# Sliding-window attention and a low-rank mixer on one core: Q and K transposed on the vector engine, scores by 64-key blocks on row tiles, batch 0 mixed d-major with a PE-added mask, loads in order of need

## The chip, the cores and the metric

The kernel runs on one core of a Trainium2 chip. The metric is the device time of one execution in microseconds (us); lower is better. A kernel was run several times, beside runs of the kernel before on the same chip, and the median is quoted. Most runs count as "fast". A run more than 1.5% above the fastest of the same kernel counts as "slow" and is left out of every comparison of times.

Engines: PE is the tensor engine (matmuls), PEld its weight loads, DVE the vector engine, ACT the scalar engine, POOL GpSimd, which issues the loads here. PSUM is the memory that PE writes its results to. "Granted clock" is the clock that the throttle gave PE, as a part of full speed.

## The reference, cut to what matters

```python
# q, k, v: (8 batches, 8 heads, 576 positions, 64), f32
scores = q @ k.T / 8                      # per batch and head
mask   = (0 <= i - j) & (i - j < 64)      # causal window of 64 positions
x      = softmax(where(mask, scores, -1e9)) @ v      # -> (8, 576, 512)
u      = x + (x.T @ U @ V).T              # U (576, 32), V (32, 576): mixes positions, low rank
out    = u + relu(u @ w_ch1) @ w_ch2      # (512, 2048) and (2048, 512)
```

There are 4608 tokens. The two large products (the MLP) work on 9 chunks of 512 tokens. A block of 64 queries sees 128 keys at most, so the attention is small, but its scores and its product with V need many small matmuls.

## The kernel before: the parts that the argument touches

All of it is one static schedule. Batch 0's attention runs alone first (the "preamble", filled up with idle matmuls). Then nine MLP chunks follow. The attention of batch c+1 is cut into pieces, and these are put by hand into the slots between the MLP steps of chunk c.

Q and K come token-major from memory and must be turned so that the head dimension lies on partitions. Before, PE does it, and ACT and DVE copy the result out of PSUM:

```python
def tr(src, j, wide=False):
    ...                                   # cut: batches 0 and 1, transposes of 96 x 96
    tp = ps_tp.tile([P, NT, P], BF16, name="tpn", tag="tp")
    for t in range(NT):                   # NT = 5; 8 calls a batch: 40 transposes
        nc.tensor.transpose(tp[:, t, :], src[:, t, 2*j : 2*j+2, :]..., ident[:])
    return ...
def TK(j): nc.scalar.copy(out=like(kt[j][:]), in_=tr(kb, j))
def TQ(j): nc.vector.tensor_copy(out=like(qt[j][:]), in_=tr(qb, j, ...))
```

The scores of a block of 64 queries are taken against a pair of key blocks (128 keys, 128 output rows), then exponentiated on ACT and multiplied by a 0/1 mask on DVE:

```python
def scores(sc, n, j, blk):
    w0 = 0 if blk == 0 else W * (blk - 1)
    for g in range(2):                    # two heads, on the two halves of PE's rows
        nc.tensor.matmul(sc[:, g, n*W:(n+1)*W],
                         kt[j][rs, w0 : w0 + P], qt[j][rs, blk*W:(blk+1)*W], ...)
def SC(j):
    ...
    nc.scalar.activation(out=dst, in_=sc[:], func=ACT.Exp, scale=scale)
    nc.vector.tensor_tensor(out=dst, in0=dst, in1=maskA..., op=ALU.mult)
```

After the low-rank product with U, batch 0 makes u token-major and turns it back, piece by piece, before the first MLP matmul can start (V: 5 products and adds, UT: transposes and copies):

```python
for part, n in (("PV", 2), ("U", 0), ("V", 0), ("UT", 0)):
    for f in a[part]:
        f()
        turn_over(n, 256)                 # idle matmuls
```

V is loaded twice, the second time shifted by 64 rows. The order of the loads is Q/K of batch 0, V of batch 0, w1, w2, then Q/K and V of batch 1.

The softmax here doesn't subtract the row's maximum and nothing guards it: scores larger than these inputs give would overflow.

Of the kernel before, what the change touches and what calls it, by code (L numbers as in the profile page):

```python
# [9 lines left out]
ALU = mybir.AluOpType  # L10
# [6 lines left out]
def kernel(  # L17
# [19 lines left out]
    HP = H // 2  # L37
# [3 lines left out]
    GR = 6  # L41
    NGR = 2
    GP = S // GR
# [14 lines left out]
    kg_pool = ctx.enter_context(tc.tile_pool(name="kg", bufs=4))  # L58
# [6 lines left out]
    ps_tp = ctx.enter_context(tc.tile_pool(name="ps_tp", bufs=1, space=bass.MemoryType.PSUM))  # L65
    first = ExitStack()
    psum = {
        "mm": first.enter_context(tc.tile_pool(name="ps_t0", bufs=2, space=bass.MemoryType.PSUM)),
        "spare": first.enter_context(tc.tile_pool(name="ps_s0", bufs=1, space=bass.MemoryType.PSUM)),
# [4 lines left out]

    ident = const.tile([P, P], BF16, name="ident")
    maskA = const.tile([P, 2, NB - 1, W], BF16, name="maskA")
    w1b = const.tile([P, NDC, F], BF16, name="w1b")
    w2b = const.tile([P, NFC, DM], BF16, name="w2b")
    NT = 5
    uf = [const.tile([P, NT, R], FP32, name=f"uf{i}") for i in range(2)]  # L80
    ub = [const.tile([P, NT, R], BF16, name=f"ub{i}") for i in range(2)]
    vrep = const.tile([P, W + S + W], BF16, name="vrep")
    vf = const.tile([P, S], FP32, name="vf")
# [3 lines left out]
    vB = [const.tile([P, NFULL, H, VW], BF16, name=f"vB{i}") for i in range(2)]  # L87
    kn = [const.tile([P, NT, H, D], BF16, name=f"kn{i}") for i in range(2)]
    qn = [const.tile([P, NT, H, D], BF16, name=f"qn{i}") for i in range(2)]
    kt = [const.tile([P, S], BF16, name=f"kt{j}") for j in range(HP)]  # L90
    qt = [const.tile([P, S], BF16, name=f"qt{j}") for j in range(HP)]
    pts = const.tile([P, HP, 2, NB, W], BF16, name="pts")

    loaded = {}


    def load_kq(b, split):
        grouped = b < NGR
        if grouped:
            kb = kg_pool.tile([GP, H, GR, D], BF16, name="kg")  # L100
            qb = kg_pool.tile([GP, H, GR, D], BF16, name="qg")
        else:
            kb, qb = kn[b % 2], qn[b % 2]
        loaded[b] = (kb, qb)
        if grouped:
            step = 2 if split else H
            for h0 in range(0, H, step):
                hs = slice(h0, h0 + step)
                for t, src in ((kb, k), (qb, q)):
                    nc.gpsimd.dma_start(  # L110
                        out=t[:, hs, :, :].rearrange("p h c d -> p h (c d)"),
                        in_=src[b, hs, :, :].rearrange("h (p c) d -> p h (c d)", c=GR),
                    )
                    yield
        else:
            for t in range(NT):
                rows = P if t < NFULL else W
                for dst, src in ((kb, k), (qb, q)):
                    nc.gpsimd.dma_start(  # L119
                        out=dst[0:rows, t, :, :],  # L120
                        in_=src[b, :, t * P : t * P + rows, :].rearrange("h p d -> p h d"),
                    )
                yield

    def load_v(b, both=False):
        va, vb = vA[b % 2], vB[b % 2]
        for t in range(NFULL):
            nc.gpsimd.dma_start(  # L128
                out=va[:, t, :, 0:D],
                in_=v[b, :, t * P : (t + 1) * P, :].rearrange("h p d -> p h d"),  # L130
            )
            if both and t > 0:
                nc.gpsimd.dma_start(  # L133
                    out=vb[:, t - 1, :, 0:D],
                    in_=v[b, :, t * P - W : t * P + W, :].rearrange("h p d -> p h d"),
                )
        lo = 0 if both else W
        nc.gpsimd.dma_start(
            out=vb[lo:P, NFULL - 1, :, 0:D],
            in_=v[b, :, NFULL * P - W + lo : S, :].rearrange("h p d -> p h d"),  # L140
        )

    def shift_v(b, copy):
        va, vb = vA[b % 2], vB[b % 2]
        for t in range(NFULL):
            if t > 0:
                copy(out=vb[W:P, t - 1, :, 0:D], in_=va[0:W, t, :, 0:D])
            copy(out=vb[0:W, t, :, 0:D], in_=va[W:P, t, :, 0:D])


    kq0 = load_kq(0, True)
    nc.vector.memset(idle[:], 0.0)  # L152
    nc.vector.memset(ident[:], 0.0)
    next(kq0)
    next(kq0)
# [9 lines left out]
    nc.vector.memset(maskA[:, 0, 0:2, :], 1.0)  # L165
    for _ in kq0:
        pass

    for n, base, step, mult in ((0, 0, 1, -1), (1, -1, -1, 1), (1, W, 1, -1)):
        nc.gpsimd.affine_select(  # L170
            out=maskA[:, 0, n, :],
            in_=maskA[:, 0, n, :],
            compare_op=ALU.is_ge,
            fill=0.0,
            base=base,
            pattern=[[step, W]],
            channel_multiplier=mult,
        )
    for i in range(2):
        nc.vector.memset(vA[i][:, :, :, D:VW], 1.0)  # L180
        nc.vector.memset(vB[i][:, :, :, D:VW], 1.0)
# [3 lines left out]
    nc.vector.memset(uf[0][:, NT - 1, :], 0.0)  # L185
    nc.vector.memset(uf[1][:, 0, :], 0.0)
    nc.vector.memset(xs[0][W:P, NT - 1, :, :], 0.0)
    nc.vector.memset(xs[1][0:W, 0, :, :], 0.0)
    for i in range(2):
        nc.vector.memset(kn[i][W:P, NFULL, :, :], 0.0)  # L190
        nc.vector.memset(qn[i][W:P, NFULL, :, :], 0.0)


    nc.sync.dma_start(
        out=uf[0][:, 0:NFULL, :], in_=moe_U[0 : NFULL * P, :].rearrange("(c p) r -> p c r", p=P)
    )
    nc.sync.dma_start(out=uf[0][0:W, NFULL, :], in_=moe_U[NFULL * P : S, :])
    nc.sync.dma_start(out=uf[1][W:P, 0, :], in_=moe_U[0:W, :])
    nc.sync.dma_start(
        out=uf[1][:, 1:NT, :], in_=moe_U[W:S, :].rearrange("(c p) r -> p c r", p=P)  # L200
    )
    for g in range(4):
        nc.sync.dma_start(out=vf[g * R : (g + 1) * R, :], in_=moe_V[:, :])
    w1v = moe_w_ch1.rearrange("(c p) n -> p c n", p=P)
    for lo, hi in ((0, 1024), (1024, 2048)):
        nc.gpsimd.dma_start(out=w1b[:, :, lo:hi], in_=w1v[:, :, lo:hi])
    shift_v(0, nc.gpsimd.tensor_copy)
    w2v = moe_w_ch2.rearrange("(i p) m -> p i m", p=P)
    for lo, hi in ((0, 8), (8, 16)):
        nc.gpsimd.dma_start(out=w2b[:, lo:hi, :], in_=w2v[:, lo:hi, :])  # L210
    for _ in load_kq(1, False):
        pass
    load_v(1, both=True)
# [10 lines left out]
    def attention(b, spare=False, alone=False):  # L224
        odd = b % 2
        kb, qb = loaded[b]
# [5 lines left out]
        grouped = b < NGR  # L232
        turn = [0]

        def tr(src, j, wide=False):
            if grouped:
                if spare and turn[0] % 3 != 0:
                    tpb = psum["mm"].tile([P, 2 * CH], BF16, name="tpm", tag="mm")
                    tp = tpb[:, 0:S].rearrange("d (c p) -> d c p", c=GR)
                elif wide:  # L240
                    tpw = ps_big.tile([P, 2, 2 * CH], BF16, name="tpw", tag="big")
                    tp = tpw[:, 0, 0:S].rearrange("d (c p) -> d c p", c=GR)
                else:
                    tp = ps_tp.tile([P, GR, GP], BF16, name="tpg", tag="tp")
                turn[0] += 1
                for c in range(GR):
                    for g in range(2):
                        nc.tensor.transpose(
                            tp[g * D : (g + 1) * D, c, :], src[:, 2 * j + g, c, :], ident[0:GP, 0:GP]
                        )  # L250
                return tp.rearrange("d c p -> d p c")
            tp = ps_tp.tile([P, NT, P], BF16, name="tpn", tag="tp")
            for t in range(NT):
                nc.tensor.transpose(  # L254
                    tp[:, t, :],
                    src[:, t, 2 * j : 2 * j + 2, :].rearrange("p h d -> p (h d)"),
                    ident[:],
                )
            return tp.rearrange("d t p -> d (t p)")[:, 0:S]

        def like(ap):
            return ap.rearrange("d (p c) -> d p c", c=GR) if grouped else ap

        def TK(j):
            def f():
                nc.scalar.copy(out=like(kt[j][:]), in_=tr(kb, j))
            return f

        def TQ(j):
            def f():  # L270
                nc.vector.tensor_copy(out=like(qt[j][:]), in_=tr(qb, j, alone and not spare))
            return f

        def scores(sc, n, j, blk):
            w0 = 0 if blk == 0 else W * (blk - 1)
            for g in range(2):
                rs = slice(g * D, g * D + D)
                nc.tensor.matmul(  # L278
                    sc[:, g, n * W : (n + 1) * W],
                    kt[j][rs, w0 : w0 + P],  # L280
# [325 lines left out]
```

## Time and profile before

Three runs before the prediction gave 350.76 to 352.54 us, median 351.7. The profiled run has a span of 349.8 us.

| part | us | what it is |
|---|---|---|
| MLP of one chunk alone | 27.6 | chunk 7, in which nothing else runs |
| preamble | 28.5 | until the first MLP matmul |
| chunks 0 and 1 | 40.2, 41.0 | with the attention of batches 1 and 2, and all first loads |
| chunks 2 to 5 | 36.5 to 37.0 | with one batch's attention and the next batch's transposes |
| chunk 6 | 34.2 | one batch's attention, no transposes |

These lines are from the page of the kernel before: PE's busy time, share and instructions; the bytes; and the chain of work that ended last, by engine.

```profile
PE 332.9 (95%) x2963; PEld 167.0 (48%) x3014; DVE 174.5 (50%) x320; ACT 125.0 (36%) x191; POOL 119.5 (34%) x150
...
HBM read 43.57 MB, written 9.44 MB: 152 GB/s over the span
...
PE 82%; DMA 9%; POOL 4%; issue 2%; ACT 1%; DVE 1%; POOLq 0%; ACTq 0%
```

PE is busy nearly throughout (95% of the span), so work that leaves PE should shorten the time. The windows view of the kernel before, cut at the first MLP matmul of each chunk, gives for each stretch its length, the busy time of PE, PEld, DVE, ACT and POOL (with instruction counts), then the granted clock, the mean DMA share and GB/s:

```profile
0.00:28.52 28.52, 22.64 (x314) 11.47 (x319) 16.16 (x43) 12.03 (x18) 22.81 (x37) 1.00 1.30 165
28.52:68.71 40.19, 37.80 (x394) 19.00 (x400) 21.29 (x36) 14.72 (x22) 25.03 (x29) 1.00 2.21 180
68.71:109.72 41.01, 38.60 (x374) 20.80 (x379) 21.14 (x40) 16.75 (x26) 33.89 (x40) 1.00 2.45 148
109.72:146.36 36.64, 36.22 (x338) 18.71 (x343) 20.10 (x36) 15.11 (x23) 15.39 (x18) 1.00 1.06 93
146.36:182.82 36.46, 36.15 (x334) 18.47 (x339) 19.92 (x36) 14.52 (x22) 15.39 (x18) 1.00 1.04 89
...
256.24:290.44 34.20, 33.84 (x298) 16.39 (x302) 18.50 (x32) 12.65 (x19) 0.00 (x0) 1.00 0.09 32
```

Chunk 6 (the last line) does an attention like that of chunk 3 (the fifth) but no transposes of a next batch, and is 2.26 us shorter. The timeline of PE in chunk 3 shows one group of transposes and two pieces of the scores (start, duration, operation, tiles, tile shape, count):

```profile
149.04 0.41 PE L278 MATMUL sc<-qt_115,kt_111 64*128 64x64 bf16 x16
149.29 0.40 PE L278 MATMUL sc<-qt_116,kt_112 64*128 64x64 bf16 x16
149.62 3.67 PE L435 MATMUL psA<-uTc,w1b 128*128 128x512 bf16 x15
...
164.28 0.45 PE L254 MATMUL tpn<-ident,kn_108 128*128 128x128 bf16 x5
164.57 0.38 PE L457 MATMUL psU<-w2b,c_4_2310 128*128 128x512 bf16 x1
```

From start to start, five transposes take 0.29 us (164.28 to 164.57), and eight such groups make 2.3 us a batch. The 32 score matmuls take 0.58 us (149.04 to 149.62), 18 ns each, weight load included.

### The profile page before, as it was taken

The page shows a single profiled execution, that of the slowest core. Times are in us where ns is not written, and L with a number is a line of the kernel's source. Part 1 is how long each engine was busy: PE and PEld are TensorE (multiplying, and loading weights), DVE is VectorE, ACT ScalarE, POOL GpSimd, SP SyncE. Part 2 cuts the span into 40 slices and gives each one's busy share as a digit, 9 for nine tenths or more (in the row PEclk, how much of TensorE's full clock was granted, in tenths as well). Part 3 has the DMA queues.
Part 4 walks back from the last instruction along what each step waited for, and adds up shares of the span by engine and source line. Part 5 has one row for each costly group of instructions (what it writes and reads, how often), then busy time and mean ns, then how long its engine had stood idle before and what let it go on. Part 6 is the DMA issues. An engine that isn't in the chain of part 4 may idle for free.

```text
span 349.8 us, 7003 instructions
## 1 busy us (share of the span) xinstructions
PE 332.9 (95%) x2963; PEld 167.0 (48%) x3014; DVE 174.5 (50%) x320; ACT 125.0 (36%) x191; POOL 119.5 (34%) x150
## 2 busy tenths in 40 slices
PE   7978989988999999999999999999999999999995
PEld 3434454444554455545554555445544454444442
DVE  3574257555653755375446545664546554214311
ACT  2632461355332632354225423353335231401300
POOL 8892269989944046605480160000000000000000
PEclk9999999999999999999999999999999999999999
DMA  8999999999999059906995292000010011011011
GB/s 112 166 207 207 198 142 188 167 171 143 149 127 167 2 37 134 187 24 45 108 163 66 15 131 66 32 2 30 32 62 0 32 43 49 0 60 62 0 52 69
DMA packets 132175, 31.89 MB, mean 91 GB/s; under 512 B 121264, under 2 KB 126384, under 8 KB 132144
## 3 DMA queue, kind: packets, MB, share of 16 engines
q0 software_dynamic: 125552, 21.57, 88.7%
q1 hardware_dynamic: 6592, 9.88, 8.2%
q8 instruction: 23, 0.38, 0.4%
q14 instruction: 8, 0.07, 0.1%
HBM read 43.57 MB, written 9.44 MB: 152 GB/s over the span
## 4 chain that ended last, share of the span: by engine, by line
PE 82%; DMA 9%; POOL 4%; issue 2%; ACT 1%; DVE 1%; POOLq 0%; ACTq 0%
PE psU L457 34%; PE psA L435 31%; DMA qg<-in_q_dram 6%; PE tpn L254 5%; PE xr L324 3%; DMA vA_103<-in_v_dram 2%; PE sc L278 2%; PE psv L373 2%; PE tpu L408 2%; PE pshh L353 1%; POOL kg L110 1%; ACT pts L293 1%; POOL qg L110 1%; POOL vA_103 L128 1%; POOL w2b L210 0%
## 5 line engine op out<-in xcount | busy, mean ns | idle before, releaser
L435 PE MATMUL psA<-uTc,w1b 128*128 128x512 bf16 x553 | 129.8, 379 | 2.1 <-ACT uTc L413 0.7
L435 PEld LDWEIGHTS <-w1b 128*128 128x128 bf16 x576 | 54.0, 98 | 62.6 <-issue 2.2
L466 DVE TENSOR_TENSOR osb<-psU,un 128x512 f32<-128x512 f32 x36 | 24.8, 690 | 60.5 <-PE psU L457 54.2
L293 ACT ACTIVATE pts<-sc 128x1024 bf16<-128x1024 f32 x32 | 31.4, 1023 | 17.9 <-PE sc L278 17.9
L294 DVE TENSOR_TENSOR pts<-pts,maskA 128x1024 bf16<-128x1024 bf16 x32 | 22.2, 695 | 17.8 <-ACT pts L293 17.6
L128 POOL DMA_DIRECT2D vA_104<-in_v_dram x16 | 14.2, 889 | 43.7 <-PE xr L324 35.7
L413 ACT COPY uTc<-tpu 128x512 bf16<-128x512 bf16 x27 | 15.8, 585 | 27.9 <-PE tpu L408 27.9
L128 POOL DMA_DIRECT2D vA_103<-in_v_dram x16 | 14.3, 907 | 17.0 <-PE xr L324 16.5
L333 DVE RECIPROCAL rcp<-xr 128x8 f32<-128x8 f32 (+1 forms) x40 | 8.2, 204 | 21.4 <-PE xr L324 21.2
L324 PEld LDWEIGHTS <-pts 128*64 128x64 bf16 x576 | 12.8, 110 | 12.2 <-issue 9.5
L119 POOL DMA_DIRECT2D kn_108<-in_k_dram x15 | 13.0, 866 | 9.0 <-PE tpn L254 8.5
L389 DVE TENSOR_TENSOR un<-psv,xs_102 128x512 bf16<-128x512 f32 (+1 forms) x18 | 11.9, 687 | 7.9 <-PE psv L373 7.9
L408 PEld LDWEIGHTS <-un 128*128 128x128 bf16 x144 | 10.6, 98 | 8.9 <-issue 1.9
L389 DVE TENSOR_TENSOR un<-psv,xs_101 128x512 bf16<-128x512 f32 (+1 forms) x18 | 11.5, 682 | 5.8 <-PE psv L373 5.8
L334 DVE TENSOR_TENSOR xs_102<-xr,rcp 128x512 bf16<-128x512 f32 (+1 forms) x20 | 13.8, 692 | 0.7
L334 DVE TENSOR_TENSOR xs_101<-xr,rcp 128x512 bf16<-128x512 f32 (+1 forms) x20 | 13.8, 690 | 0.7
L500 PE MATMUL unread<-idle 128*128 128x256 bf16 (+1 forms) x46 | 12.5, 371 | 1.6 <-DVE idle L152 1.3
L119 POOL DMA_DIRECT2D kn_107<-in_k_dram x15 | 12.9, 863 | 3.2 <-PE tpn L254 2.5
L119 POOL DMA_DIRECT2D qn_110<-in_q_dram x15 | 13.1, 874 | 1.4 <-PE tpn L254 1.4
L119 POOL DMA_DIRECT2D qn_109<-in_q_dram x15 | 13.0, 867 | 1.2 <-PE tpn L254 0.9
L373 PE MATMUL psv<-hh,vrep 128*128 128x512 bf16 x40 | 12.7, 379 | 0.7 <-DVE un L389 0.6
L133 POOL DMA_DIRECT2D vB_106<-in_v_dram x12 | 10.7, 892 | 6.2 <-DMA w2b<-in_moe_w_ch_dram 4.2
(579 smaller groups left out, 590.8 us busy)
## 6 DMA issues: line engine op xcount, KB each, us to landing
out_dram<-osb SPq DMA_DIRECT2D x36, 256.0 KB, 2.6
vA_103<-in_v_dram POOLq DMA_DIRECT2D x16, 128.0 KB, 6.0
w1b<-in_moe_w_ch_dram POOLq DMA_DIRECT2D x2, 1024.0 KB, 13.7
w2b<-in_moe_w_ch_dram POOLq DMA_DIRECT2D x2, 1024.0 KB, 15.3
vA_104<-in_v_dram POOLq DMA_DIRECT2D x16, 128.0 KB, 5.7
vB_106<-in_v_dram POOLq DMA_DIRECT2D x16, 128.0 KB, 5.9
kn_107<-in_k_dram POOLq DMA_DIRECT2D x12, 128.0 KB, 5.5
qn_109<-in_q_dram POOLq DMA_DIRECT2D x12, 128.0 KB, 5.6
```

The lines of the kernel that those rows point to most:

```text
L119: nc.gpsimd.dma_start(out=dst[0:rows, t, :, :], in_=src[b, :, t * P : t * P + rows, :].rearrange("h p d -> p h d"),)
L128: nc.gpsimd.dma_start(out=va[:, t, :, 0:D], in_=v[b, :, t * P : (t + 1) * P, :].rearrange("h p d -> p h d"),)
L293: nc.scalar.activation(out=dst, in_=sc[:], func=ACT.Exp, scale=scale)
L294: nc.vector.tensor_tensor(out=dst, in0=dst, in1=maskA.rearrange("p g n w -> p g (n w)"), op=ALU.mult)
L324: nc.tensor.matmul(xr[r0 : r0 + W, h // 4, (h % 4) * VW : (h % 4 + 1) * VW], pts[:, h // 2, h % 2, blk, :], rhs, start=True, stop=True,)
L334: nc.vector.tensor_tensor(out=x[lo:hi, t, :, :].rearrange("p (a h) d -> p a h d", a=2), in0=xv[:, :, :, 0:D], in1=rcp[lo:hi].to_broadcast( ...
L373: nc.tensor.matmul(ps[:, n, :], vrep[:, off : off + P], hh["sb"][:], start=True, stop=not on_pe)
L389: nc.vector.tensor_tensor(out=u_tiles[g][rs, :], in0=ps[rs, n, :], in1=xt[n][rs], op=ALU.add)
L408: nc.tensor.transpose(tp[:, dc, :], u_tiles[g][:, dc * P : (dc + 1) * P], ident[:])
L435: nc.tensor.matmul(ps[:], w1b[:, dc, i * P : (i + 1) * P], uTc[:, dc, :], start=(dc == 0), stop=(dc == NDC - 1),)
L457: nc.tensor.matmul(acc[t][:], c1[i][:, t * P : (t + 1) * P], w2b[:, i, :], start=(i == 0), stop=(i == NFC - 1),)
L466: nc.vector.tensor_tensor(out=osb[:], in0=acc[t][:], in1=u_tiles[g][:], op=ALU.add)
```

## The change

The intent is to take everything off PE that another engine can do, and to start the MLP sooner:

1. Q and K are loaded in runs such that DVE's transpose instruction (STREAM_TRANSPOSE in the profile; the kernel arranges its operands in blocks of 32x32) gives the wanted layout. PE's transposes and the copies out of PSUM go.
2. The scores are taken by single 64-key blocks, against up to 128 queries at once: 80 matmuls a batch on 64x64 tiles instead of 72 on 64x128.
3. Batch 0's mask is added in PSUM by PE before the exponential. Batch 0's result is built d-major in PSUM (features on partitions, as the MLP needs it: x transposed plus the product of V and the low-rank part), so that no turning back is needed; its token-major u follows in chunk 0.
4. V is loaded once, and shifted by copies on DVE. Loads are issued in order of need.

The diff, cut to its core:

```diff
-        tp = ps_tp.tile([P, NT, P], BF16, name="tpn", tag="tp")
-        for t in range(NT):
-            nc.tensor.transpose(tp[:, t, :], src[:, t, 2*j : 2*j+2, :]..., ident[:])
+    def KT(x, n):                        # batches 0 and 1: as pairs, in 32-bit elements
+        if pair:
+            nc.vector.transpose(out=dst[...].bitcast(U32)..., in_=src[...].bitcast(U32)...)
+        else:
+            nc.vector.transpose(out=dst[:, n * S : (n + 1) * S]..., in_=src[...]...)
 ... (cut)
+    def SC0(n):                          # batch 0: mask first, on PE
+        for g in range(2):
+            nc.tensor.matmul(sc[:, g, 0 : PB * W], ident[:], bias[...], start=True, stop=False)
+        ...                              # then the scores, accumulated onto it
+    def SC(n):
+        if alone:
+            return SC0(n)
+        for r in range(max(len(x) for x in todo)):
+            for e in range(ne):          # ne = 2 where Q/K lie as pairs (batch 1), else 1
+                for half in range(2):
+                    jj, kb, a, z = todo[half][r]
+                    for g in range(2):
+                        nc.tensor.matmul(
+                            sc[half * W : (half + 1) * W, g, (a - lo) * W : (z - lo) * W],
+                            operand("k", g, jj, e, kb * W, (kb + 1) * W),
+                            operand("q", g, jj, e, ...), ...)
 ... (cut)
+    def XT(t):   # x transposed into PSUM, left open
+    def UP():    # plus (low-rank part) @ V, then four copies to the MLP's operand
 ... (cut)
-    DVE_RELU = (1, 2, 3, 5, 6, 7, 9, 11)
+    DVE_RELU = (1, 4, 7, 10, 13)
 ... (cut: new slots)
+    PLACE   = {"VC": [0], "S": [1, 1, 4, 4, 7, 7], "PV": [10, 10, 13, 13, 15],
+               "KT": [8, 9, 11, 12, 14, 16, 18, 19], ...}
+    PLACE_1 = {"KT": [14, 15, 17, 18], "S": [17, 17, 19, 19, 21, 21], "VC": [23], ...}
+    KT_3    = [22, 23, 24, 25, 26, 27, 29, 30]
+    turn_over(88, P)                     # idle matmuls of 128 columns at the start
 ... (cut)
+            place(b + 1, ("KT",), {"KT": KT_3} if b == 2 else PLACE)
```

"KT" is the list of slots of the DVE transposes of the next batch. In the last line, chunk 1 places batch 3's transposes late (slots 22 to 30), and all later chunks use slots 8 to 19.

## The prediction

> **What bounds the kernel now.** The page gives PE 95% busy at full granted clock; the chain that ended last is 82% PE. In the timeline MLP matmuls (128x512) follow each other every 0.216 us, so a chunk of 128 costs 27.6 us. Nine chunks are 249 of the 349.8 us span, untouched by the change. The rest, by stage (windows view):
> - preamble (batch 0's attention), to the first MLP matmul: 28.5 us, bound by dependencies and DMA. From the last low-rank matmul (22.6) to that MLP matmul it is 5.5 us.
> - chunks 0 and 1: 40.0 and 41.4 us, 12 to 14 above the floor.
> - chunks 2 to 5: 36.4 to 37.0 us each; chunk 6: 34.2; chunks 7 and 8: the floor, plus a 4 us tail.
> Chunk 6 differs from 2-5 only in having no Q/K transposes of a next batch, so these cost PE about 2.3 us a batch (40 transposes, start to start 55 ns: 2.2 us).
>
> **What changes.**
> 1. Q/K transposes leave PE for DVE. Gain 2.2 us in each of chunks 2-5, about 4.5 in chunk 1, which does two batches. New: 8 DVE transposes of 576 elements. [...] Removed: 4 q copies (0.45 us) on DVE, 4 k copies on ACT (0.65), three of eight DVE relus (0.69). Added: V shifts, about 1.5 us. [...]
> 2. Scores: 72 matmuls of 64 columns (1.7 us of PE a batch) become 80, mostly of 128 columns, on four 64x64 tiles. If four run at once [...], PE cost stays 1.5-2 us; if only two do, 2.8.
> 3. V is loaded once, not twice; Q and K descriptors become 512 B, or 4.6 KB for batches 0 and 1 (but from batch 2 each byte of Q and K is fetched twice).
> 4. Batch 0: 4 Q/K loads instead of 8, no PE transposes or PSUM copies, mask in PSUM, result built d-major, so after U come hh copy, 4 matmuls and 2 copies per engine: about 2.2 us instead of 5.5. MLP starts near 22 instead of 28.5. Its u adds (5 matmuls, 1.1 us) move into chunk 0.
> 5. Loads in order of need: batch 1's Q/K (landed at 45.2 us now, and waited for) come before the second half of w2; I estimate 37 us at the 0.4 MB/us that w2 reached.
>
> **Sum.** Preamble -6.5, chunk 0 -2.5, chunk 1 -5, chunks 2-5 -1.8 each = -7, chunk 6 +0.3: about -21 us, nearly all on the critical path, because PE is the chain there. The ideal without new waits is -24. Predicted 331 us, 8 in 10 between 324 and 340. Chances: faster 0.95, within 2% 0.04, slower 0.01.
>
> **What would show it.** First MLP matmul at 21-23 us; chunks 2-5 of 34.3-35.2 us; [...] no PE waits over 0.5 us after chunk 1; the DMA share near full through chunks 0 and 1; two score pieces taking 0.5-0.65 us between MLP matmuls.
>
> **What would make it wrong.** Batch 2's Q/K (4.7 MB of reads, each DMA writing only 32 partitions) landing late, so that DVE blocks in order behind its transposes and chunk 1 waits 5 us or more; w1 or w2 late, since MLP starts 6.5 us sooner with the same bytes to fetch; transposes twice as slow; score tiles running in pairs only (+1 us a batch).

The sum came to about -21 us (-6.5, -2.5, -5, -7, +0.3); DVE's work entered it only in that DVE was taken not to be a bound. Measured, a bf16 transpose took 0.79 us in the mean, and DVE's busy time in chunks 2 and 3 went from 20.10 and 19.92 to 24.45 and 23.18 us. The V shifts, an estimate of 1.5 us, took 1.65 (0.68 and 0.97 at 100.51). The 1.5-2 and 2.8 us for the scores are estimates (from start to start a batch took 1.37 us before and takes 1.40 now); that four tiles run at once was an assumption, which e11 tests.

## The result, and the profile after

| kernel | median us | lowest to highest | runs |
|---|---|---|---|
| before | 351.92 | 350.76 to 352.54 | 4 |
| after | 336.47 | 335.85 to 337.35 | 4 |

The ratio is 0.9562, with a 95% interval of 0.953 to 0.9595: faster. Ratios here and below compare fast runs, and are not quite the ratio of the medians.

The prediction of 331 us (324 to 340) holds the measured 336.47. The gain was 15.4 us and not 21. That the range held it owes something to its width of 16 us: stage by stage, as the table below shows, misses of 10.3 us stood against 3.5 us more than predicted elsewhere. The page of the kernel after, the lines that answer those of before:

```profile
PE 317.6 (95%) x2848; PEld 156.1 (47%) x2891; DVE 195.8 (58%) x343; ACT 118.3 (35%) x188; POOL 87.9 (26%) x116
...
HBM read 51.30 MB, written 9.44 MB: 181 GB/s over the span
...
PE 57%; DMA 29%; DVE 7%; POOL 3%; issue 2%; ACT 0%; DVEq 0%; POOLq 0%
```

PE's busy time fell by 15.3 us and the span by 14.1. V is read once, but from batch 2 on Q and K are read twice, so 51.3 MB are read instead of 43.6. The chain that ended last now goes through DMA for 29%, against 9%. That is not the price of the bytes: e1 below reads the same 51.3 MB, and DMA has 2% of its chain. It is the wait of chunk 2, shown next, that leads the chain back into the loads. The windows view of the kernel after, in the same columns:

```profile
0.00:25.79 25.79, 20.88 (x392) 15.48 (x393) 15.98 (x42) 7.80 (x10) 17.93 (x32) 1.00 1.29 163
25.79:65.76 39.97, 36.82 (x389) 17.75 (x396) 26.41 (x43) 12.89 (x21) 17.38 (x21) 1.00 1.72 185
65.76:99.68 33.92, 33.39 (x301) 16.14 (x306) 27.42 (x47) 13.57 (x22) 16.71 (x20) 1.00 2.48 161
99.68:138.80 39.12, 35.84 (x309) 16.79 (x311) 24.45 (x41) 14.88 (x24) 17.05 (x21) 0.96 2.24 151
138.80:173.01 34.21, 33.77 (x302) 16.14 (x306) 23.18 (x40) 13.71 (x22) 14.67 (x18) 1.00 1.49 149
...
242.19:276.33 34.14, 33.88 (x306) 16.39 (x310) 18.37 (x32) 14.29 (x23) 0.00 (x0) 1.00 0.09 32
```

Set side by side, with the terms of the prediction (stage lengths in us, after minus before; "c0" is chunk 0):

| | preamble | c0 | c1 | c2 | c3 to c5 | c6 | c7, c8 | sum |
|---|---|---|---|---|---|---|---|---|
| predicted | -6.5 | -2.5 | -5 | -1.8 | -5.4 | +0.3 | 0 | -21 |
| measured, this profile | -2.73 | -0.22 | -7.09 | +2.48 | -6.49 | -0.06 | 0 | -14.1 |

Chunks 1 and 3 to 5 did better than predicted. The preamble, chunk 0 and chunk 2 fell short, by 3.8, 2.3 and 4.3 us. So three questions are left: what keeps the preamble long, what eats the gain of chunk 0, and why chunk 2 alone is 5 us longer than its like.

In the preamble, PE's timeline of the kernel after shows a hole that no dependence explains:

```profile
18.19 0.20 PE L375 MATMUL xr<-vA,pts 128*64 128x65 bf16 x1
20.17 0.33 PE L588 MATMUL xT<-idle 128*128 128x128 bf16 x3 [1.79 <-issue]
...
25.79 1.46 PE L513 MATMUL psA<-uTc,w1b 128*128 128x512 bf16 x6 [0.61 <-DVE uTc L492]
```

PE stands 1.79 us before an idle matmul on constant data. "issue" says that the profile knows nothing that it waited for.

In chunk 2, DVE's timeline of the kernel after shows a real wait:

```profile
111.50 0.82 DVE L243 STREAM_TRANSPOSE kt<-kr 128x576 bf16<-128x576 bf16 x1 [1.16 <-DMA vB<-in_v_dram]
114.05 0.81 DVE L243 STREAM_TRANSPOSE qt<-qr 128x576 bf16<-128x576 bf16 x1 [1.72 <-DMA qr<-in_q_dram]
```

And PE's timeline of the same microseconds:

```profile
116.44 0.22 PE L375 MATMUL xr<-vA,pts 128*64 128x65 bf16 x1 [2.02 <-DVE xs L385]
117.41 0.22 PE L375 MATMUL xr<-vA,pts 128*64 128x65 bf16 x1 [0.52 <-DVE xs L385]
```

DVE runs its instructions here in the order of the program. At 111.5 and 114.05 it stands before transposes of batch 4, which nobody needs until the next chunk (the last K load of batch 4 landed at 111.31 and the last Q load at 113.83 us; that the profile names V's DMA at 111.5 is its guess), and behind them wait a relu and the scaling of x ("xs") that PE needs for the current batch. The windows view of these microseconds shows what PE made of it, and what the clock did then:

```profile
114.00:118.00 4.00, 1.46 (x35) 0.79 (x34) 3.82 (x8) 0.21 (x1) 1.62 (x2) 1.00 2.69 124
118.00:120.00 2.00, 1.82 (x5) 0.69 (x5) 1.97 (x5) 0.49 (x1) 0.81 (x1) 0.53 2.36 151
```

PE was busy for 1.46 of 4 us, and in the next 2 us the granted clock was 0.53: six MLP matmuls took 2.69 us from start to start (118.36 to 121.05), 0.45 us each and not 0.216. The stall is paid for twice.

### The profile page after: what moved, and what is told of

The parts are those of the page before. It is cut to its first block, busy times and chain, and to the rows that moved or that the text cites. A ratio compares the mean times of both kernels' runs of the same rounds, so it can differ in the third digit from the quotient of the medians.

```text
span 335.7 us, 6763 instructions
## 1 busy us (share of the span) xinstructions
PE 317.6 (95%) x2848; PEld 156.1 (47%) x2891; DVE 195.8 (58%) x343; ACT 118.3 (35%) x188; POOL 87.9 (26%) x116
## 4 chain that ended last, share of the span: by engine, by line
PE 57%; DMA 29%; DVE 7%; POOL 3%; issue 2%; ACT 0%; DVEq 0%; POOLq 0%
PE psU L535 27%; PE psA L513 24%; DMA qr<-in_q_dram 13%; DMA vA<-in_v_dram 12%; DMA kr<-in_k_dram 4%; PE xr L375 2%; PE sc L341 2%; PE tpu L451 2%; DVE un L431 2%; DVE qt L243 2%; DVE xs L385 1%; DVE osb L544 1%; POOL kr L112 1%; PE pshh L401 1%; PE psv L420 1%
## 5 line engine op out<-in xcount | busy, mean ns | idle before, releaser
L535 PE MATMUL psU<-w2b,c 128*128 128x512 bf16 x558 | 133.2, 379 | 1.7 <-issue 1.0
L524 ACT ACTIVATE c<-psA 128x512 bf16<-128x512 f32 x99 | 59.3, 599 | 100.5 <-PE psA L513 99.9
L535 PEld LDWEIGHTS <-c 128*128 128x128 bf16 x576 | 53.3, 98 | 59.9 <-issue 3.3
L522 DVE TENSOR_SCALAR c<-psA 128x512 bf16<-128x512 f32 x45 | 30.7, 682 | 36.6 <-PE psA L513 36.5
L124 POOL DMA_DIRECT2D vA<-in_v_dram x32 | 29.0, 911 | 46.5 <-PE xr L375 26.8
L349 ACT ACTIVATE pts<-sc 128x768 bf16<-128x768 f32 x42 | 31.7, 808 | 12.5 <-PE sc L341 10.6
L456 ACT COPY uTc<-tpu 128x512 bf16<-128x512 bf16 x30 | 17.6, 585 | 41.0 <-PE tpu L451 41.0
L356 DVE TENSOR_TENSOR pts<-pts,mask 128x768 bf16<-128x768 bf16 x42 | 23.3, 558 | 11.8 <-ACT pts L349 8.3
L385 DVE TENSOR_TENSOR xs<-xr,rcp 128x512 bf16<-128x512 f32 (+1 forms) x40 | 27.6, 691 | 1.4
L112 POOL DMA_DIRECT2D kr<-in_k_dram x24 | 19.7, 820 | 29.2 <-DMA vA<-in_v_dram 10.6
L431 DVE TENSOR_TENSOR un<-psv,xs 128x512 bf16<-128x512 f32 (+1 forms) x40 | 25.1, 678 | 3.8 <-PE psv L420 3.3
```

The source lines that it names most:

```text
L112: nc.gpsimd.dma_start(out=dst[32 * part : 32 * (part + 1), off : off + NJJ * RD].rearrange("p (n x) -> p n x", x=r * D), in_=src[b, m * NJ ...
L124: nc.gpsimd.dma_start(out=va[:, t, :, 0:D], in_=v[b, :, t * P : (t + 1) * P, :].rearrange("h p d -> p h d"),)
L349: nc.scalar.activation(out=dst, in_=sc[:, :, 0 : PB * W].rearrange("p g (n w) -> p g n w", w=W), func=ACT.Exp, scale=scale,)
L385: nc.vector.tensor_tensor(out=x[lo:hi, t, :, :].rearrange("p (a h) d -> p a h d", a=2), in0=xv[:, :, :, 0:D], in1=rcp[lo:hi].to_broadcast( ...
L431: nc.vector.tensor_tensor(out=u_tiles[g][rs, :], in0=ps[rs, n, :], in1=xt[n][rs], op=ALU.add)
L522: nc.vector.tensor_relu(out=c1[i][:], in_=ps[:])
```

## The experiments

Twelve kernels were run. All were correct. "Before" in each is the kernel before on the same chip.

| run | median us (lowest to highest) | ratio to before, 95% interval | preamble, c0, c1, c2 in its profile |
|---|---|---|---|
| a0_after | 336.03 (335.74 to 338.22) | 0.9565, 0.9525 to 0.9606 | 28.31, 39.98, 33.92, 34.99 |
| e1_kt4_late | 333.19 (332.67 to 335.87) | 0.9486, 0.944 to 0.9533 | 26.96, 39.98, 33.92, 34.15 |
| e2_pair3 | 337.21 (334.12 to 340.89) | 0.9519, 0.9471 to 0.9567 | 25.55, 39.97, 39.70, 34.99 |
| e3_fewer_idle | 340.03 (335.51 to 341.95) | 0.9623, 0.9549 to 0.9696 | slow |
| e8_late_align | 333.95 (332.65 to 334.56) | 0.9477, 0.9433 to 0.952 | 27.57, 40.38, 33.92, 34.14 |
| e10_late_align_kt1 | 332.96 (331.86 to 333.57) | 0.9451, 0.9401 to 0.9502 | 27.30, 38.80, 33.92, 34.14 |
| e14_late_kt1 | 334.47 (333.46 to 335.74) | 0.951, 0.947 to 0.955 | 25.27, 42.07, 35.31, 34.14 |
| e15_late_kt1_shift72 | 333.2 (332.49 to 333.8) | 0.9479, 0.9454 to 0.9504 | 27.36, 38.81, 33.92, 34.15 |
| e9_loads_later | 338.4, one run | | 25.97, 45.69, 33.92, 34.15 |
| e11_late_halves | 334.14, one run | | 26.55, 40.54, 33.99, 34.22 |
| e12_late_token_major | 339.45, one run | | 31.47, 41.29, 33.92, 34.14 |
| e13_late_dve_mask | 334.78, one run | | 27.92, 40.22, 33.92, 34.14 |

The medians of e2 and e3 include a slow run each; those of their three fast runs are 335.66 and 339.9 us.

### a0: the kernel after, again

The edit is none. It shows how much one kernel's profile moves, and stands beside e1, e2 and e3 on one chip.

> The changed kernel itself, as the base of the runs that follow on this chip. Both theories: 336.5 us within 1, stages as in its first profile: first MLP matmul at 25.8 us, chunks 40.0, 33.9, 39.1, 34.2, 35.0, 34.2, 34.1, 27.6. Open: whether the 1.8 us hole of PE at 18.3 us (no wait on a semaphore) and the stall of chunk 2 come back at the same places.

It took 336.03 us. The stages of its profile are the same to 0.01 us in chunks 0, 1 and 3 to 7, but the preamble was 28.31 instead of 25.79, and chunk 2 34.99 instead of 39.12. So of the three stages that fell short, two vary from run to run. A single profile of them proves little; only a mechanism that is there in every profile does, or a timed comparison.

### e1: batch 4's transposes in late slots

```diff
-                place(b + 1, ("KT",), {"KT": KT_3} if b == 2 else PLACE)
+                place(b + 1, ("KT",), {"KT": KT_3} if b in (2, 3) else PLACE)
```

The theory is that DVE stands in order behind transposes whose loads are late. The rival is that DVE has too much work in chunk 2. The edit moves eight transposes 11 to 14 slots later within the same chunk; DVE's work in the chunk stays the same.

> Only the place of batch 4's Q/K transposes in chunk 2 is changed: slots 22 to 30 instead of 8 to 19. Theory A (chunk 2 is long because DVE, which works in order, stands at transposes whose loads are late, and so holds back what frees PE's PSUM buffers, after which PE also runs at a lower granted clock): chunk 2 falls from 39.1 to 34.2-35.0 us, its clock is 1.00 again, total -4.5 us, 332.0. Rival B (DVE has too much work in chunk 2, 24.5 us, the late loads are incidental): the same work is still there, only later, and collides with the adds of the up-projection: chunk 2 stays above 37.5, total at best -1.5.

The windows view of e1, chunks 1 and 2:

```profile
66.94:100.86 33.92, 33.92 (x307) 16.14 (x306) 27.50 (x47) 13.56 (x22) 17.27 (x21) 1.00 2.42 165
100.86:135.01 34.15, 34.15 (x314) 16.38 (x312) 24.13 (x41) 14.88 (x24) 13.97 (x18) 1.00 2.39 164
```

In chunk 2, PE is busy for all of 34.15 us, at full clock, with DVE's busy time as before (24.13 against 24.45 us). In the timeline the transposes now run from 126.5 us on, and none waits for a load. By time, e1 is 0.9486 against a0's 0.9565 of before, 0.8% or about 2.8 us (the difference of these two, times 351.5); the intervals just touch.

This profile alone doesn't prove the cure, for a0 had no stall either. The landing of batch 4's last Q load, counted from the start of chunk 2, decides it. With the early slots it landed at -4.6 us in e2 and 9.7 in a0, and chunk 2 took 34.99 us in both; at 14.2 in the kernel after and 18.1 in e3, and PE waited 2.0 and 5.9 us for DVE. In e1 it happened to land at 10.5. But with the same late slots it landed at 14.2 in e11, 15.7 in e10 and 17.6 in e14, and there was no stall: in all nine profiles with late slots chunk 2 took 34.14 to 34.22 us. Here is e14's, in the windows view:

```profile
102.65:136.79 34.14, 34.14 (x313) 16.34 (x311) 24.94 (x42) 14.88 (x24) 15.18 (x19) 1.00 1.90 149
```

So the theory of too much work falls, and the in-order wait stands: the stall grows with the lateness of the load, and only where the transposes are early.

### e2: batch 2 loaded once, in pairs

```diff
-    RUN = [RP, RP] + [2] * (B - 2)
-    PAIRED = [True, True] + [False] * (B - 2)
+    RUN = [RP] * 3 + [2] * (B - 3)
+    PAIRED = [True] * 3 + [False] * (B - 3)
```

Batch 4's loads might be late because the double reading of batches 2 and 3 fills the queue ahead of them. This edit takes away the double reading of batch 2, at the price of 160 score matmuls for it instead of 80.

> Batch 2 is loaded and transposed as batches 0 and 1 are: each byte of Q and K read once (2.4 MB less), in long runs, with 32-row score tiles in two passes. Theory C (the queue of DMA work, swollen by reading Q and K twice, is what makes batch 4's loads late in chunk 2): everything behind it arrives 6 us or so sooner, chunk 2's stall goes (39.1 to about 34.5), while chunk 1 pays for the two-pass scores, +1.2 us; total -3.4, 333.1. Rival D (the loads are late because they are issued late, at slot 13 of chunk 1, not because the DMA engines are full): chunk 2 stays near 39, total +1.2.

Chunk 2 was 34.99 us, without the stall. But a0, with all its double reading, had 34.99 too, so the length of the chunk tells nothing about why batch 4's loads came late. Their times do: at the same place in the program they were issued from 74.9 us on and the last Q landed at 100.6, against 84.5 and 113.8 in the kernel after. Chunk 1 took 39.70 instead of 33.92 us, in part through another hole of the preamble's kind (3.03 us, ending at 85.52, "issue") and a clock of 0.96. One of its runs was slow; by the ratio, 0.9519, it lies between a0 and e1, with intervals that overlap both (the mean of its three fast runs is 336.2, of a0's four 336.5). So the place of issue in the program is not the whole cause, and batch 2's double loads hold batch 4's back. Whether by their bytes, their number (8 loads for 4) or the buffer, which batch 2's transposes left at 75.7 us and not at 79.7, one profile does not separate.

### e3: fewer idle matmuls

```diff
-    turn_over(88, P)
+    turn_over(22, CH)
-    turn_over(16, P)
+    turn_over(4, CH)
```

Now the hole in the preamble. It stood, in the kernel after, behind the 352nd weight load that the trace shows; in a0, e1, e2, e11 and e14, whose instructions are the same up to there, it is at the same instruction (2.06, 1.79, 2.01, 2.06 and 1.47 us). My theory: PE had run out of fetched instructions. The rival: something in the work at that place. e3 gives PE the same idle columns (104 times 128 are 26 times 512) in a quarter of the idle matmuls, 156 instructions fewer. A fetch theory lets the hole move to another instruction; a cause in the work leaves it where it is.

> The 104 idle matmuls of 128 columns at the start become 26 of 512: the same PE time, 156 PE instructions fewer. Theory F (PE's hole of 1.8 us at 18.3 us is a wait for its own instructions to be fetched while the DMA engines are full): the hole goes or moves, first MLP matmul 1 to 1.8 us sooner. Rival G (a dependence that the trace does not show): the hole stays before the same idle matmul, first MLP matmul at 25.8 within 0.3.

The hole moved, to a matmul of the product with V that waits for nothing:

```profile
18.08 0.19 PE L375 MATMUL xr<-vA,pts 128*64 128x65 bf16 x1 [2.52 <-issue]
```

In e3's stream this is after 224 weight loads, where the others stood after 352: 128 pairs of a weight load and a matmul apart, which is 256 instructions. The trace has a DMA queue named "instruction" (q8); in the kernel after it carried 22 packets of 16,384 bytes (0.36 MB on the page) for PE's 2848 matmuls and 2891 weight loads, one for some 260 of them, and after each crossing of such a boundary there is one packet. In the kernel after, PE crossed the boundary of 224 weight loads at about 14.0 us, the packet came between 17.5 and 18.0, and PE, which had used up the next 256 instructions by 18.19, went on at 20.17.

The profiled run of e3 counts as slow, so its times are not used to say that e3 is worse. But its profile shows no slower chip: chunk 1 and chunks 3 to 7 are the same to 0.01 us as in a0, and what is longer is chunk 2, 42.61 us, with the DVE stall of the kernel after at 5.9 us. It is used above for this stall alone.

### e8 and e15: other places for the boundary

```diff
-    turn_over(88, P)
+    turn_over(24, P); turn_over(16, CH)       # e8, with e1's edit
```
```diff
-    turn_over(88, P)
+    turn_over(40, P); turn_over(12, CH)       # e15, with the edits of e1 and e14
```

If the hole is a late block, then a boundary put where PE works through large matmuls should cost less. Both shift the boundaries against the work.

> Batch 4's transposes late (as before), and the 88 idle matmuls of 128 columns become 24 of 128 and 16 of 512: same PE time, 96 PE instructions fewer. Theory F (PE's instructions come in blocks of 256, each asked for when the block before is entered, and usable some 6 us later in this busy stretch; the hole is what is left of the 6 us when PE has run through a block sooner): the boundaries now fall near the second burst of idle matmuls (10 us), near the fourth or last score piece (15.3 us) and in the MLP; the hole is about 0.9 us, at 15.3, and none at 18.3. First MLP matmul at 24.6-25.2 us at full clock, total 331.0. Rival (the holes depend on DMA traffic alone, not on the count): hole of 1.8 to 2.5 us somewhere between 15 and 20 us, first MLP matmul at 25.5 to 28, total as with batch 4's transposes late, 333.

> The same with 36 idle matmuls fewer at the start (40 of 128 columns and 12 of 512, equal PE time), so that PE's block boundaries fall at about 9.6, 15.0 and 22 us. If a block costs 6 to 7 us from the boundary before it, as seen so far, the hole is 0.8 to 1.5 us, at 15.0, [...] and the first MLP matmul comes at 25.0 us; total 330.5. If the hole is 2 us again, wherever the boundary falls, counting instructions is no remedy and the total is that of the run beside it within 0.5%.

The timeline of PE in e8:

```profile
17.39 0.64 PE L299 MATMUL sc<-qt,kt 32*64 32x128 bf16 x21 [2.34 <-issue]
```

And in e15:

```profile
16.60 0.48 PE L282 MATMUL sc<-bias,ident 128*128 128x384 bf16 x1 [2.10 <-issue]
```

The hole moved again, as a fetch theory says, but it did not shrink: I expected 0.9 us in e8 and 0.8 to 1.5 in e15, and measured 2.34 and 2.10. The numbers of three kernels tell why. From the crossing to the resumption it took 6.2 us in the kernel after (14.0 to 20.17), 6.1 in e3 (12.0 to 18.08) and 6.8 in e8 (10.6 to 17.39). PE used up its 256 instructions in 4.2 to 4.5 us in the first and the last. As long as small matmuls follow for those 256 instructions, the hole is the difference, wherever it lies. (Crossing times are read to 0.4 us, so these are rough.) In e8, e10, e13 and e15 the hole stands behind the 224th weight load, as in e3. The kernel before, whose PE took 17 us from its 224th weight load (18.2) to its 352nd (35.4), had the block's packet at 20.85 and has no such hole.

### e9: the loads moved away from the hole

```diff
-    load_w1(0, 512) ... load_w1(512, 1024) ... load_w1(1024, 2048); load_w2(0, 8)
-    load_kq(1); load_w2(8, 16); load_v(1); ...
+    nc.gpsimd.tensor_copy(out=gate[0:W, :], in_=xs[0][0:W, NT - 1, 0, :])   # after batch 0's PV
+    (the same loads here)
```

This is e1's PE stream, instruction for instruction, but all later loads wait until batch 0's product with V is done. If the block is late because the DMA engines are full, there is no hole now; if a refill simply takes 6 us, it stays.

> Slower on purpose: all weights, batch 1 and U's second half are loaded only after batch 0's last PV, so that the DMA engines are idle while PE runs the preamble; PE's instructions are those of the changed kernel. If the 6 us from asking to having a block of instructions are due to the loads in flight, the block comes sooner and the hole at 18.3 us is under 0.3. If they are a fixed latency, the hole stays at 1.8 to 2 us. First MLP matmul near 27 to 30 us, total 340 to 350 either way.

PE runs through at 18.2 us. Its timeline has two short waits around there:

```profile
14.21 0.40 PE L298 MATMUL sc<-qt,kt 32*64 32x128 bf16 x19 [0.33 <-issue]
16.82 0.27 PE L471 MATMUL xT<-ident,xs 128*128 128x128 bf16 x2 [0.32 <-ACT pts L306]
```

PE came to the place at the same time as in the kernel after (18.3 us) and went on. The instruction packet for the boundary crossed at 14.0 us came between 15.0 and 15.5, against 17.5 to 18.0 with the loads; from 17 to 20 us the DMA engines moved one packet, of instructions, 1.4 us after the next boundary was crossed at 18.3 us (with the loads it took 5.7 us). The d-major product ended at 22.3 instead of 24.15 us. So the hole is an instruction block that comes late through DMA engines busy with loads; of the twelve runs this is the one that shows the cause, in one profile. The price, as had to be: the first MLP matmul waited 2.62 us for w1 (25.97 us), and chunk 0 took 45.69. It is no better kernel.

### The clock behind the hole

The profiles of a0, after, e1, e2, e11 and e14 have the same preamble, and their first MLP matmul came at 28.31, 25.79, 26.96, 25.55, 26.55 and 25.27 us. The windows view gives their mean granted clock until then as 0.88, 1.00, 0.94, 1.00, 0.94 and 1.00. With 1.00 it is at most 25.79; the rest is the clock, which fell to half in the hole or behind it (e1: 0.58 and 0.56 in the windows view of 20 to 22 and 22 to 24 us). The traces' clock records give the spells exactly: 0.50 for 6.83 us from 19.48 in a0, for 3.41 us from 20.34 in e1 and from 19.52 in e11. In the kernel after, whose preamble has none, the one spell within the span is that behind the stall of chunk 2: 0.50 for 3.41 us from 118.10. Halving is what these runs show. The length of the hole alone does not decide it: behind holes of 2.06 us (a0), 1.79 (e1) and 2.06 (e11) the clock fell, and behind 1.79 (after), 2.01 (e2) and 1.47 (e14) it did not. The four spells named here are 3.41 or 6.83 us long. What sets one off and what sets its length, no run here shows, so that stays open.

### e10 and e14: batch 1's transposes earlier

```diff
-        "KT": [14, 15, 17, 18],
+        "KT": [12, 13, 14, 15],
```

e14 is e1 with this edit; e10 is e8 with it. It is about chunk 0. There, in the kernel after, PE waited 1.02 us at 46.42 for the last transpose of batch 1 on DVE (which had come behind the first mask multiplications, at 45.11), and 0.76 us at 52.16 for the shift of V.

> The same, with batch 1's transposes at slots 12 to 15 of chunk 0 instead of 14 to 18. If chunk 0 waits 1.0 us because DVE came to the fourth transpose only after the first masks, and not because batch 1's loads were late (they had landed by 38.2 us), that wait goes and V's wait with it: chunk 0 from 40.0 to 38.8 us, total 329.9. If V of batch 1, landing near 50.6 us, is what chunk 0 waits for in the end, chunk 0 stays at 39.5 or more.

> Both places changed, and nothing else: batch 4's transposes in slots 22 to 30 of chunk 2, batch 1's in slots 12 to 15 of chunk 0; the start is that of the changed kernel. From the runs so far the parts should add: chunk 0 38.8, chunk 2 34.15, first MLP matmul between 25.5 and 28.3 us (hole of 1.8 to 2.1 us at 18.2 us, clock after it halved or not), total 331.7 median, 15.5% less preamble noise not expected. If the parts don't add (the loads of batches 2 and 3 fall behind the earlier chunks), chunk 1 or 2 grows by over 1 us and the total stays at 333.

In e10 (and in e15) the first of the two waits is gone and chunk 0 takes 38.80 us, 1.2 less. In e14 chunk 0 took 42.07. Its PE timeline says why:

```profile
25.27 6.21 PE L513 MATMUL psA<-uTc,w1b 128*128 128x512 bf16 x28 [0.61 <-DVE uTc L492]
52.30 0.65 PE L375 MATMUL xr<-vB,pts 128*64 128x65 bf16 x8 [2.60 <-DVE vB L136]
```

Its MLP had started 2.03 us sooner than e10's (27.30). But V of batch 1 landed when it landed: DVE's shift at 51.55 had waited 1.75 us for that DMA, PE waited 2.60 us, and the clock fell to 0.57 for 52 to 56 us. Chunk 0 ended at 67.34 us in e14 and at 66.10 in e10, and in no run before 65.5. So once the transposes are early, V's load is the next bound, and time won in the preamble is given back there. This is one profile, in which the last load of V that the shift needs landed at 51.53 us, against 50.34 in the kernel after and 49.96 in e10 (but 51.50 in e12); how much of it is the rule, the run does not say. Chunk 1 grew too, to 35.31 us, which the expectation had named as the sign that the parts don't add: DVE waited 1.13 and 0.43 us there for loads. The times agree in direction (0.951 against 0.9451 of before), with intervals that overlap.

### e11: score tiles in two instead of four

```diff
-                for r in range(...):
-                    for e in range(ne):
-                        for half in range(2):
+                for half in range(2):
+                    for r in range(...):
+                        for e in range(ne):
```

The prediction rested on four 64x64 tiles running at once, which no run had shown. With this order (on top of e1) only two tiles alternate at any time. If four do run at once in the kernel after, this should cost about double.

> Batch 4's transposes late, and in each score piece all matmuls into PSUM partitions 0 to 63 come before those into 64 to 127, so that only two of the four 64x64 tiles can be at work at a time; same instructions, other order. If four tiles at once are what keeps the scores' PE time at 1.4 us a batch with 128 columns instead of 64, two score pieces take 0.75 us or more instead of 0.46 and each undisturbed chunk (4 and 6) grows by 0.7 to 1.0 us, from 34.2 to about 35. If the issue of instructions bounds them, the chunks stay at 34.2.

PE's timeline of the kernel after, two pieces of the scores and the MLP matmul behind them:

```profile
101.50 0.54 PE L341 MATMUL sc<-qt,kt 64*64 64x128 bf16 x26
101.97 2.76 PE L513 MATMUL psA<-uTc,w1b 128*128 128x512 bf16 x11
```

The same in e11:

```profile
209.63 0.55 PE L341 MATMUL sc<-qt,kt 64*64 64x64 bf16 x26
210.11 2.76 PE L513 MATMUL psA<-uTc,w1b 128*128 128x512 bf16 x12
```

From start to start it is 0.47 us in the one and 0.48 in the other for 26 matmuls; the chunks got 0.07 us longer. So on 64x64 tiles the order hardly matters: 18 ns a pair of weight load and matmul here, and 18 ns in the kernel before, on tiles of twice the width and half the columns. A batch took 1.37 us before (0.58, 0.57 and 0.22) and takes 1.40 now (0.47, 0.46 and 0.47).

That is no rule for all tiles. The edit also reorders batch 1's scores in chunk 0, which use 32x64 tiles. The kernel after:

```profile
48.79 0.78 PE L341 MATMUL sc<-qt,kt 32*64 32x64 bf16 x56
49.50 1.90 PE L535 MATMUL psU<-w2b,c 128*128 128x512 bf16 x7
```

The same in e11:

```profile
49.95 1.11 PE L341 MATMUL sc<-qt,kt 32*64 32x64 bf16 x56
50.99 1.25 PE L535 MATMUL psU<-w2b,c 128*128 128x512 bf16 x4
```

Here 56 matmuls take 0.71 us with four tiles in turn and 1.04 with two, and another group of 48 takes 0.69 and 0.98. So a pair costs 13 to 14 ns there in the one order, and 19 to 20 in the other: the order does matter there, and 18 ns is no fixed price. (Batch 1's matmuls also add in pairs into one place of PSUM, and the edit moves the two from four matmuls apart to two, so the number of tiles is not singled out.) What sets the 18 ns on 64x64 tiles stays open.

### e12 and e13: batch 0 token-major again, and the mask on DVE again

e12 (on top of e1) undoes the d-major build: V and UT run before the first MLP matmul again, and not in chunk 0. e13 (on top of e1) undoes the mask in PSUM:

```diff
-            if alone:
-                return SC0(n)                  # e13
```

> Batch 0's result goes the old way (up-projection token-major, 5 adds, 4 groups of PE transposes and copies) and its adds are not in chunk 0. If the d-major way is what shortens the stretch from the low-rank matmuls to the MLP (4.2 us in the changed kernel, 6.9 in the one before), the first MLP matmul comes 2 to 3 us later than with batch 4's transposes late alone, which was 26.96 us at 0.94 clock, chunk 0 falls by 1.1 to 1.5 us, and the sum is 1 to 1.5 us worse. If copies and adds overlap as well the old way, the sum is unchanged.

> Batch 0's scores masked on DVE after the exponential, as in all other batches, and no mask matmuls on PE (12 of 384 columns, 2.6 us of PE). If the mask in PSUM takes 6 x 0.56 us off the DVE queue where that queue is the chain (transposes, V shifts, PV's scaling), the first MLP matmul comes 1 to 2.5 us later than 26.96. If PE or the hole of instruction fetch is the chain there, it comes within 0.5 us of it or sooner.

In e12 the first MLP matmul came at 31.47 us, 4.5 later than in e1 (I had expected 2 to 3), and the whole took 339.45 us, 6.3 more than e1's median (I had expected 1 to 1.5). It had the same hole (2.27 us) and a clock of 0.86 over the preamble, so a part of the 4.5 is the clock. Chunk 0 did not get shorter in return (41.29, with waits and a clock of 0.94). The d-major build is worth having; one run does not give its size.

In e13 the first MLP matmul came at 27.92 us against 26.96, and the whole took 334.78 us. The spread of one and the same preamble is 25.3 to 28.3 us, so the worth of the mask in PSUM is not shown.

### The best version

e10 has the lowest median, 332.96 us, a ratio of 0.9451 to the kernel before, against 0.9562 for the kernel after: 3.5 us by the medians. Its interval overlaps with those of e1, e8 and e15. The part that is shown is e1's edit, one line: all five timed kernels with it have lower medians than the kernel after and a0 (332.96 to 334.47 against 336.47 and 336.03), and chunk 2 does not stall in any of their profiles.

## Why the prediction was right or wrong

**PE's transposes, right, and worth a little more than written.** "Gain 2.2 us in each of chunks 2-5": chunks 3 and 5 went from 36.46 to 34.21, by 2.25 us, and chunk 4 by 1.99. Chunk 6, which had no transposes before, stayed (34.20 to 34.14). I had then taken off 0.4 us a chunk for new costs, and there were none. Chunk 1 lost 7.09 instead of 5: two batches' transposes (4.6) and a wait of the kernel before, 1.70 us at 79.43 for a copy of a transposed Q, which went with them and which I had not counted. The remaining 0.8 I have not itemised.

**The scores, right in size, the mechanism not confirmed.** Two pieces take 0.47 us, near the predicted 0.5 to 0.65. But on the 64x64 tiles that I had costed, the order of the tiles, four in turn or two, made no difference (e11, 0.47 and 0.48 us): 80 matmuls with more columns cost what 72 did, at 18 ns a pair in both. "If only two do, 2.8" came out only for batch 1's 32x64 tiles, and there in part: 1.04 us for 0.71.

**DVE's transposes.** Of bf16 elements they took 0.79 us in the mean (791 and 797 ns on the page, 48 of them); what I had put on them rested on no run. Of batches 0 and 1, which go in 32-bit elements, they took 1.25 us for the same 576 elements, here from DVE's timeline of the kernel after:

```profile
5.87 1.25 DVE L235 STREAM_TRANSPOSE kt<-kr 128x576 uint32<-128x576 uint32 x1
9.27 1.25 DVE L235 STREAM_TRANSPOSE kt<-kr 128x576 uint32<-128x576 uint32 x1 [1.02 <-DMA kr<-in_k_dram]
```

There are four of them at the head of the preamble, 0.46 us longer each than those of bf16. But each starts within 0.4 us of the landing of its load (loads landed at 5.51, 6.97, 9.24 and 10.64 us; the transposes start at 5.87, 6.99, 9.27 and 10.67), so only the last one can have cost the path its 0.46 us.

**The preamble, the step that failed most: -6.5 predicted, -2.73 measured.** I had written "MLP starts near 22 instead of 28.5". Of these 6.5 us, 3.3 were to come after the low-rank product ("about 2.2 us instead of 5.5"), and 3.2 before it. In these terms, counted from the end of the last low-rank matmul, the stretch took 5.53 us before (22.99 to 28.52) and 3.30 after (22.49 to 25.79): a gain of 2.2. (The copy of the low-rank result took 0.8 us of the 3.30, the 4 products 0.86, and the copies to the MLP's operand, with the wait for them, 1.64.) Before it, only 0.5 was gained, and the first low-rank matmul did not start sooner at all (21.66 and 21.64). The loads of Q and K did land sooner, the last at 10.64 us and not at 13.22. What ate 1.8 of the missing 2.7 us is a term that I did not have: PE standing for a block of instructions that was behind the loads in the DMA engines (e3 and e9; in e9 the low-rank product starts at 19.82). The last 32-bit transpose can account for 0.46 more; I have not itemised the rest. The clock behind such a hole then adds 0 to 2.5 us by chance. The idle matmuls of 128 columns, which I took as free, are also instructions to fetch; that fewer of them help was not shown (e3, e8, e15).

**Chunk 0: -2.5 predicted, -0.22 measured.** Batch 1's scores are taken in two halves of the head dimension: 160 matmuls, 2.55 us by PE's timeline (0.69, 1.15 and 0.71), not the 1.5 to 2 that I gave a batch. PE waits 1.02 us for a transpose that I had not seen standing behind the masks (e10 takes this away: -1.2), and 0.76 for V's shift, which e10 still has.

**Chunk 2: -1.8 predicted, +2.48 in this profile, -1.65 in that of a0.** I had named the mechanism, "DVE blocks in order behind its transposes", as a danger for batch 2 in chunk 1. It came for batch 4 in chunk 2, in two of the four profiles with the early slots. "No PE waits over 0.5 us after chunk 1" was wrong with 2.02. That it is the place of the transposes in DVE's order is shown by e1's edit, over all profiles with and without it.

**Loads.** "The DMA share near full through chunks 0 and 1" was right, and too short: it stays at 90% or more, in the slices of the page, to about 176 us, against 114 before. I put this down to the double reading of Q and K, and to it that a slot that was good in the steady state (8 to 19) was too early in chunk 2; e2 supports it in one profile and does not single out the bytes.

Of the 15.4 us gained, the chunks 1 and 3 to 5 gave 13.6 in this profile, nearly all of it PE's transposes and the wait for one of their copies. Of the 5.6 us missing against the prediction, the edits of e1 and e10 bring back some 3.5. What is left lies in the preamble and, with 1.1 us, in chunk 0.

## What to carry to other kernels

Work moved from the engine that is the bottleneck to an idle engine gained here what it cost from start to start (2.25 us a chunk in chunks 3 and 5, for transposes that took 2.3). But DVE ran its instructions in order, and PE waited 2.02 us for it in chunk 2: put a piece that waits for a load behind all that the current stage needs, above all where the DMA engines are full. Measure what a pair of tiny matmul and weight load costs on the tiles in use (13 to 20 ns here) before counting on columns or tiles. A stream of them also needs new blocks of instructions, which came late here while the DMA engines were full (PE went on 6.1 to 6.8 us after the crossing; without the loads, in e9, the packet came 1.0 to 1.5 us after it): a wait that the profile calls "issue", at the same count of instructions in every run, is worth checking against that. Before shortening a preamble, look where the next load lands: e14 began 2 us sooner than e10 and ended chunk 0 1.2 us later.
